# Seven half-size products for one more group: sums, a held-back unit and a moved load in a linear-attention and feed-forward kernel

## The chip, the core and the metric

The kernel runs on one core of a Trainium2 chip. The core has a matrix engine (TensorE, PE in the profile; its weight loads are PEld), a vector engine (VectorE, DVE), a scalar engine (ScalarE, ACT), GpSimd (POOL) and SyncE (SP), which here issues nearly all DMAs. Each engine works through its own instructions in program order and waits on semaphores for the others. The metric is the device time of one execution in microseconds.

## The reference

Eight batches of attention with a linear kernel, followed by a two-layer feed-forward network on all 4608 tokens:

```python
def phi(x, c, s):                       # c, s: cos and sin of the position
    r = np.maximum(x, 0.0)
    return np.concatenate([r * c, r * s], axis=-1)
q_p, k_p = phi(q, cos_w, sin_w), phi(k, cos_w, sin_w)   # (8, 8, 576, 64) -> (..., 128)
kv  = np.einsum('bhsf,bhsd->bhfd', k_p, v)
z   = np.sum(k_p, axis=2)
num = np.einsum('bhsf,bhfd->bhsd', q_p, kv)
den = np.einsum('bhsf,bhf->bhs', q_p, z)[..., None] + 1e-06
x   = (num / den).transpose(0, 2, 1, 3).reshape(4608, 512)
h   = x @ w_in                          # 512 -> 2048
g   = np.maximum(0.01 * h, h)
out = g @ w_out                         # 2048 -> 512
```

## The kernel before

The tokens are cut into nine groups of 512, counted from 0: groups 0 to 7 hold the first 512 tokens of batches 0 to 7, group 8 the 64 tokens that are left of every batch. Both weight matrices are kept in SBUF in 16 bits (`w1`, `w2`).

For every batch b the steps are: load k, v and q (`load_kv`, `load_main`, DMAs on SP's queue into a pool of five staging buffers); build k's features, 9 tokens with a cosine and a sine half each (`k_cos`, `k_sin`, L267 on VectorE or L265 on ScalarE, tile kp); cast v (`v_pairs`); sum k and v into kv on TensorE (`kv_sum`, L366, 72 small matmuls, with a copy on ScalarE); build q's features in four parts j (`q_prep`, tile qp) and transpose them by DMA in two halves (`q_transpose_dma`, L401); for each j multiply with kv (`num`, L432) and divide on VectorE (`divide`: den, rden, xs, L443 to L448); and transpose x by DMA (`x_transpose_dma`, L413). `num` and `kv_sum` share the one buffer of the PSUM pool `ps_n`.

For every group g the first product (`ffn1`, L504) has 16 units of four 512-wide matmuls. Two units fill one buffer of the pool `ps_h`, which has two, and ScalarE takes them through the leaky ReLU into the tile g (L512).

The second product has two forms. Groups below `G7` (3 before) take 16 units of four 512-wide matmuls (`ffn2`, L527), and each four units end in one copy from PSUM (`ffn2_out`) and a store. Groups from `G7` on use Strassen's scheme in Winograd's form: g is cut into quarters a11, a12, a21, a22 (two halves of the tokens, even and odd slices of the 2048 features), `w2` into b11, b12, b21, b22, and seven products of half the size take the place of eight. A product is two units of eight 256-wide matmuls (`ffn2s`, L610), 14 units in all, in the order 1, 6, 2, 7, 5, 4, 3. They accumulate in three chains, each in one bank of the pool `ps_o`, which has two banks: X holds products 1 and 2, Y holds 6, 7 and 4, Z holds 5 and 3. Between two products of a chain the sum so far is read out: t1 after product 1 (ScalarE), t2 after 6, t3 after 7 (adds on VectorE, L552), and an output quarter after 2 (ScalarE), 5, 4 and 3 (VectorE).

The operands are made on VectorE (`tt_op`, L552) by `g_sum`: S1 = a21 + a22 and S2 = S1 - a11; a21 becomes a11 - a21, and a12 becomes a12 - S2 after product 2. `weight_sum` makes T1, T2 and T4 in buffers of their own, and number 3 overwrites b12 in `w2` by b22 - b12, so that it has to stand behind the last group that uses `w2` as it is. Product 7 multiplies the new a21 with the new b12; product 6 is S2 by T2, product 5 S1 by T1.

The order is written out by hand. From group 1 on, a list of units (`order`, L856 to L871) holds for each g the units of the second product of g and those of the first product of g+1: `ahead` units of the second product first (15 for group 1, 8 for group 2, none for 3 to 7), the rest spread between the first product's units by `behind`. The n-th entry of the list of g has the place 16 g + 16 n / (length of the list). The steps of the batches have fixed places (L903 to L946), and `weave` puts a step ahead of the first unit whose place is not below the step's. So a list with more entries moves the steps against the units. Steps near the change: q of batch 4 from 30, k from 31, the `num` of batch 3 at 27.5, 28.6, 29.7 and 30.8, its x transpose at 31.4, q transposes of batch 4 at 31.6 and 33.2, loads of k and v of batch 5 at 31.7 and 33.4, v casts of batch 4 on ScalarE at 32.5 and 33.5, the kv sum of batch 4 at 36.

Of the kernel before, what the change touches and what calls it, by code (L numbers as in the profile page):

```python
# [20 lines left out]
def kernel(  # L21
# [27 lines left out]
    NFT = DFF // P  # L49
    NG = B + 1  # L50
    NE = D + 2
    G7 = 3

    ctx.enter_context(tc.manual_schedule())

# [21 lines left out]
    def psum(where, shape, dtype, name):  # L77
        p = {"h": ps_h, "o": ps_o, "n": ps_n}[where]
        return p.tile(shape, dtype, name=name, tag="ps_" + where)

    st = {}
    ACT, DVE, POOL = nc.scalar, nc.vector, nc.gpsimd
# [56 lines left out]
    for i in range(DFF // 512):  # L139
        for c in range(0, NKC, 2):  # L140
            n = 1 if i == 0 and c == 0 else 2
# [353 lines left out]
    def ffn1(g, m, lo=0, hi=MAIN, chunks=range(NKC), where="h"):  # L495

        if ("g", g) not in st:
            st["g", g] = gpool.tile([P, NFT, MAIN], dt.float16, name="g")
        if m % 2 == 0 and chunks[0] == 0 and lo == 0:
            st["h", m // 2] = psum(where, [P, 2, MAIN], dt.float32, "ps_h")  # L500
        xT = st["xT", g]
        ps = st["h", m // 2]
        for c in chunks:
            nc.tensor.matmul(  # L504
                ps[:, m % 2, lo:hi],
                lhsT=w1[m // 4, c][0][:, w1[m // 4, c][1], m % 4 : 512 : 4],
                rhs=xT[:, lo // P : hi // P, c, :],
                start=(c == 0 and lo == 0),
                stop=(c == NKC - 1 and hi == MAIN),
            )  # L510
        if m % 2 == 1 and chunks[-1] == NKC - 1 and hi == MAIN:
            nc.scalar.activation(st["g", g][:, m - 1 : m + 1, :], ps, AF.Lrelu)  # L512
            if g >= G7 and m == NFT - 1:
                for n in (1, 2):
                    g_sum(g, n, NPR // 2, NPR)

    def ffn2(g, i, eng=DVE):
        tt, part = divmod(i, 4)
        if part == 0 and ("ps_o", g, tt) not in st:
            st["ps_o", g, tt] = psum("o", [P, DM], dt.float32, "ps_o")  # L520
        ffn2_mm(g, tt, 4 * part, 4 * part + 4)
        if part == 3 and eng is not None:
            ffn2_out(g, tt, eng)

    def ffn2_mm(g, tt, lo, hi):
        for m in range(lo, hi):
            nc.tensor.matmul(  # L527
                st["ps_o", g, tt],
                lhsT=st["g", g][:, m, tt * P : (tt + 1) * P],
                rhs=w2[:, m, :],  # L530
                start=(m == 0),
                stop=(m == NFT - 1),
            )
# [5 lines left out]
    NPR, HT, HC = NFT // 2, 2 * P, DM // 2  # L539
# [11 lines left out]
    def tt_op(o, a, b, op):  # L551
        nc.vector.tensor_tensor(out=o, in0=a, in1=b, op=op)  # L552

    def weight_sum(n):
        b11, b12, b21, b22 = (w2q[:, e, c] for e in range(2) for c in range(2))
        if n == 1:
            tt_op(T1, b12, b11, ALU.subtract)
        elif n == 2:
            tt_op(T2, b22, T1, ALU.subtract)
        elif n == 4:  # L560
            tt_op(T4, b21, T2, ALU.subtract)
        else:
            tt_op(b12, b22, b12, ALU.subtract)

    def g_quarter(g, r, e, lo=0, hi=NPR):
        gv = st["g", g].rearrange("p (i e) t -> p e i t", e=2)
        return gv[:, e, lo:hi, r * HT : (r + 1) * HT]

    def g_sum(g, n, lo, hi):
        a11, a12, a21, a22 = (  # L570
            g_quarter(g, r, e, lo, hi) for r in range(2) for e in range(2)
        )
        if n == 1:
            tt_op(S1[:, lo:hi], a21, a22, ALU.add)
        elif n == 2:
            tt_op(S2[:, lo:hi], S1[:, lo:hi], a11, ALU.subtract)
        elif n == 3:
            tt_op(a21, a11, a21, ALU.subtract)
        else:
            tt_op(a12, a12, S2[:, lo:hi], ALU.subtract)  # L580

    def product(g, n):

        return {
            1: (g_quarter(g, 0, 0), w2q[:, 0, 0]),
            2: (g_quarter(g, 0, 1), w2q[:, 1, 0]),
            3: (g_quarter(g, 0, 1), w2q[:, 1, 1]),
            4: (g_quarter(g, 1, 1), T4),
            5: (S1, T1),
            6: (S2, T2),  # L590
            7: (g_quarter(g, 1, 0), w2q[:, 0, 1]),
        }[n]
# [4 lines left out]
    def ffn2s(g, u):  # L597
        n, tt = ORDER7[u // 2], u % 2
        a, b = product(g, n)
        key = "ps7", g, CHAIN[n]  # L600
        apart = g == NG - 1 and CHAIN[n] == "Z"
        if apart:
            key = *key, tt
        first = key not in st
        if first:
            where = "n" if g == NG - 1 and key[2] == "Y" else "h" if apart else "o"
            st[key] = psum(where, [P, 2, HC], dt.float32, "ps_7")
        ps = st[key]
        for i in range(NPR):
            nc.tensor.matmul(  # L610
                ps[:, tt],
                lhsT=a[:, i, tt * P : (tt + 1) * P],
                rhs=b[:, i],
                start=(first and i == 0),
                stop=(i == NPR - 1 and (apart or tt == 1)),
                skip_group_check=True,
            )
        if apart:
            part = slice(tt * HC, (tt + 1) * HC)
            osb = out_tile(g, HC)  # L620
            tt_op(osb, ps[:, tt], {5: t3, 3: t2}[n][:, part], ALU.add)
            store_tail(2 * (n == 5) + tt, 1, osb)
        if apart or tt == 0:
            return
        flat = ps.rearrange("p t c -> p (t c)")
        if n == 1:
            nc.scalar.copy(t1, flat)
        elif n == 6:
            tt_op(t2, flat, t1, ALU.add)
        elif n == 7:  # L630
            tt_op(t3, flat, t1, ALU.add)
        else:
            osb = out_tile(g, 512)
            if n == 2:
                nc.scalar.copy(osb, flat)
                g_sum(g, 4, 0, NPR)
            else:
                tt_op(osb, flat, {5: t3, 4: t1, 3: t2}[n], ALU.add)
            r, c = {2: (0, 0), 5: (1, 1), 4: (1, 0), 3: (0, 1)}[n]
            store_quarter(g, r, c, osb.rearrange("p (t c) -> p t c", t=2))  # L640

    def out_tile(g, n):
        if g == NG - 1:
            return stage.tile([P, n], dt.float32, name="osb", tag="stage")
        return opool.tile([P, n], dt.float32, name="osb", tag="osb")
# [29 lines left out]
    def ffn2_out(g, tt, eng):  # L675
        ps = st["ps_o", g, tt]
        osb = opool.tile([P, DM], dt.float32, name="osb", tag="osb")
        copy(eng, osb, ps)
        rows = out[g * S : g * S + MAIN, :].rearrange("(p j) d -> p j d", j=J)
        if g == 0:  # L680
            held.append((rows[:, tt, :], osb))
        else:
            nc.sync.dma_start(rows[:, tt, :], osb)
# [43 lines left out]
    for m in range(2):  # L727
        ffn1(0, m, 0, half, range(0, 1))
    num_half(0, 0, 1, None, ps)
    for m in range(2):  # L730
        ffn1(0, m, 0, half, range(1, 2))
# [37 lines left out]
    def f1(g, m, where="h"):  # L769
        return lambda: ffn1(g, m, where=where)  # L770

    def f2(g, i):
        return lambda: ffn2s(g, i) if g >= G7 else ffn2(g, i)

    steps = []

    def at(pos, f, *args):
        steps.append((pos, lambda: f(*args)))
# [26 lines left out]
    order = [(tt, part) for part in range(3) for tt in range(J)]  # L805
# [47 lines left out]
    for g in range(1, NG):  # L853
        last = 14 if g >= G7 else 16
        ahead = {1: 15, 2: 8, NG - 1: last}.get(g, 0)
        order = [f2(g, i) for i in range(ahead)]  # L856
        left = last - ahead
        behind = [
            0 if g == 1 else -(-16 * (k + 1) // left) - 1 for k in range(left)
        ]  # L860
        for i in range(16 if g + 1 < NG else 0):
            order.append(f1(g + 1, i))
            order += [f2(g, ahead + k) for k in range(left) if behind[k] == i]
            if i == 11 and g + 1 >= G7:
                order.append(lambda g=g: [g_sum(g + 1, n, 0, NPR // 2) for n in (1, 2, 3)])
        if g == G7 - 1:
            order.append(lambda: weight_sum(3))
        if g + 1 >= G7 and g + 1 < NG:
            order.append(lambda g=g: g_sum(g + 1, 3, NPR // 2, NPR))
        for n, u in enumerate(order):  # L870
            units.append((16 * g + 16 * n / len(order), u))  # L871

# [14 lines left out]
    def load_steps(b, pk, pv, pq):  # L887
        at(pk, load_kv, "k", k, b)
        at(pv, load_kv, "v", v, b)
        at(pq, load_main, "q", q, b)  # L890
# [30 lines left out]
    kv_steps(4, 31, 0.5, 36, ACT)  # L921
    out_steps(4, 37.3, 1.4, 1.2)

    load_steps(5, 31.7, 33.4, 25)
    for j in range(J):
        at(39 + 1.4 * j, q_prep, 5, j)
    for jp in range(2):
# [51 lines left out]
```

## Time and profile before

| | before |
|---|---|
| median of 3 runs | 285.25 us (285.19 to 285.26) |
| profiled execution | 285.09 us, span 283.3 us |
| busy: TensorE | 275.4 us, 97% of the span |
| busy: VectorE | 165.9 us, 59% |
| busy: ScalarE | 130.5 us, 46% |
| DMA | 57.53 MB, mean 203 GB/s |
| second product, 512-wide matmuls (L527) | 192, 379 ns each |
| second product, 256-wide matmuls (L610) | 672, 273 ns each |
| second product of group 2, first eight units | 97.19 to 104.10 us |

The durations of matmuls overlap their neighbours, since TensorE pipelines them: a unit of four 512-wide matmuls takes 0.86 us from start to start, not four times 379 ns. The chain of work that ended last counts them without the overlap, and is the view to cost TensorE by. In VectorE's timeline the next instruction also starts before the one ahead has quite ended, so a row is costed by the distance to the next row. A row gives its start, its duration, its engine and line, what it writes and reads, and in brackets how long the engine was idle ahead of it and what ended that.

### The profile page before, as it was taken

To read this page: it belongs to the slowest core of one execution; us is meant where nothing else is said; L and a number is where in the kernel's file an instruction comes from. 1 tells how busy PE (TensorE), PEld (TensorE's weight loads), DVE (VectorE), ACT (ScalarE), POOL (GpSimd) and SP (SyncE) were. 2 spreads that over 40 slices of the span, in tenths; PEclk is the share of its full clock that TensorE was granted. 3 is DMA by queue.
4 is the path that set the end of the run, shared out by engine and by line. 5 is a ranking of instruction groups with operands and counts; after the bars stand their busy time and mean duration, and the time that the engine had idled before them with its cause. 6 is when DMAs were issued, how large, how long until landed. Compare 5 with 4: busy or idle time off the path is not lost.

```text
span 283.3 us, 5818 instructions
## 1 busy us (share of the span) xinstructions
PE 275.4 (97%) x2442; PEld 177.7 (63%) x2442; DVE 165.9 (59%) x394; ACT 130.5 (46%) x175; POOL 11.5 (4%) x23
## 2 busy tenths in 40 slices
PE   7899999999999999999999999999999999999993
PEld 2585455555446555556777777767776677667882
DVE  5940597955993883856675567555556514324452
ACT  6856366572037524784493449343334242332300
POOL 2056000000000000000000000000000000000000
PEclk9999999999999999999999999999999999999999
DMA  7999999699999999799599919441496052111124
GB/s 225 335 384 415 377 398 372 182 221 306 238 247 308 382 192 280 238 210 328 204 191 353 265 49 185 99 125 40 108 190 149 2 111 76 38 39 36 38 79 110
DMA packets 78202, 57.53 MB, mean 203 GB/s; under 512 B 50400, under 2 KB 66784, under 8 KB 77792
## 3 DMA queue, kind: packets, MB, share of 16 engines
q1 hardware_dynamic: 77568, 56.63, 72.7%
q10 hardware_dynamic: 608, 0.52, 0.6%
q8 instruction: 19, 0.31, 0.5%
q14 instruction: 7, 0.06, 0.1%
HBM read 36.70 MB, written 9.44 MB: 163 GB/s over the span
## 4 chain that ended last, share of the span: by engine, by line
PE 93%; DMA 2%; SPq 1%; ACT 1%; DVE 1%; issue 0%; DVEq 0%
PE ps_h L504 44%; PE ps L610 26%; PE ps_o L527 15%; PE ps_kv L366 3%; PE ps_num L432 3%; DMA vst<-in_v_dram 2%; SPq L115 1%; PE ps_xth L484 1%; PE ps_qt L422 1%; SPq L105 1%; PE ps_numh L468 1%; PE ps_idle L187 0%; ACT qpT L273 0%; DVE xT L829 0%; DVE xs L448 0%
## 5 line engine op out<-in xcount | busy, mean ns | idle before, releaser
L504 PE MATMUL ps_h<-xT,w 128*128 128x512 f16 (+1 forms) x592 | 141.3, 374 | 0.1
L512 ACT ACTIVATE g<-ps_h 128x1024 f16<-128x1024 f32 x72 | 73.1, 1023 | 92.2 <-PE ps_h L504 92.1
L504 PEld LDWEIGHTS <-w 128*128 128x128 f16 x592 | 64.7, 114 | 41.1 <-DMA xT<-xs 0.3
L610 PEld LDWEIGHTS <-g 128*128 128x128 f16 x480 | 46.5, 98 | 14.1
L610 PE MATMUL ps<-w,g 128*128 128x256 f16 x384 | 48.8, 273 | 0.0
L527 PE MATMUL ps_o<-w,g 128*128 128x512 f16 x192 | 45.0, 379 | 0.0
L527 PEld LDWEIGHTS <-g 128*128 128x128 f16 x192 | 18.3, 98 | 20.5
L610 PE MATMUL ps<-T,ext 128*128 128x256 f16 x192 | 24.6, 273 | 0.0
L610 PEld LDWEIGHTS <-ext 128*128 128x128 f16 x192 | 18.5, 98 | 5.3
L443 DVE TENSOR_SCALAR den<-ps_num 128x8 f32<-128x8 f32 x28 | 4.6, 164 | 28.7 <-PE ps_num L432 28.5
L552 DVE TENSOR_TENSOR ext<-g 128x1024 f16<-128x1024 f16 x12 | 8.2, 687 | 22.1 <-ACT g L512 22.1
L552 DVE TENSOR_TENSOR ext<-ps,ext 128x512 f32<-128x512 f32 x12 | 8.3, 692 | 21.1 <-PE ps L610 21.1
L552 DVE TENSOR_TENSOR osb<-ps,ext 128x512 f32<-128x512 f32 (+1 forms) x20 | 12.7, 635 | 13.5 <-PE ps L610 13.4
L448 DVE TENSOR_TENSOR xs<-ps_num,rden 128x512 f16<-128x512 f32 x28 | 19.4, 691 | 1.0
L267 DVE TENSOR_SCALAR kp<-kst,sin_t 128x256 f16<-128x256 f32 x54 | 17.9, 347 | 0.0
L267 DVE TENSOR_SCALAR qp<-qst,cos_t 128x512 f16<-128x512 f32 (+1 forms) x34 | 15.5, 457 | 3.2 <-DMA qst<-in_q_dram 3.2
L265 ACT ACTIVATE kp<-kst,cos_t 128x256 f16<-128x256 f32 (+1 forms) x35 | 15.9, 489 | 1.2 <-DMA kst<-in_k_dram 1.2
L267 DVE TENSOR_SCALAR qp<-qst,sin_t 128x512 f16<-128x512 f32 (+1 forms) x34 | 15.5, 457 | 0.0
L432 PEld LDWEIGHTS <-qpT 128*128 128x128 f16 (+1 forms) x256 | 10.6, 101 | 5.4 <-issue 1.2
L610 PE MATMUL ps<-ext,g 128*128 128x256 f16 x96 | 12.3, 273 | 0.0
L432 PE MATMUL ps_num<-kv,qpT 128*128 128x66 f16 (+1 forms) x256 | 11.8, 194 | 0.0
L273 ACT CAST vm<-vst 128x1152 f16<-128x1152 f32 x10 | 11.3, 1147 | 0.3 <-DMA vst<-in_v_dram 0.3
(83 smaller groups left out, 182.5 us busy)
## 6 DMA issues: line engine op xcount, KB each, us to landing
out_dram<-osb SPq DMA_DIRECT2D x32, 256.0 KB, 2.9
qst<-in_q_dram SPq DMA_DIRECT2D x7, 1024.0 KB, 8.1
kst<-in_k_dram SPq DMA_DIRECT2D x6, 1152.0 KB, 9.5
vst<-in_v_dram SPq DMA_DIRECT2D x5, 1152.0 KB, 8.4
w2st<-in_moe_w_out_dram SPq DMA_DIRECT2D x3, 1024.0 KB, 13.4
ext<-in_moe_w_in_dram SPq DMA_DIRECT2D x4, 512.0 KB, 11.1
w1st<-in_moe_w_in_dram SPq DMA_DIRECT2D x3, 512.0 KB, 9.9
kst<-in_k_dram SPq DMA_DIRECT2D x2, 576.0 KB, 12.4
```

What stands on the lines that cost most here:

```text
L265: nc.scalar.activation(o, i, AF.Relu, scale=col)
L267: eng.tensor_scalar(out=o, in0=i, scalar1=0.0, scalar2=col, op0=ALU.max, op1=ALU.mult)
L273: nc.scalar.copy(o, i)
L366: nc.tensor.matmul(ps[:, o, (c - lo) * NE : (c - lo + 1) * NE], lhsT=st["kp", b][sl, c, j, :], rhs=vm[b % 2][sl, c, j, :], start=(j == 0), ...
L432: nc.tensor.matmul(ps[lo:hi, h // 4, (h % 4) * NE : (h % 4 + 1) * NE], lhsT=qpT[:, h, lo:hi], rhs=kv[b][:, h, :],)
L443: nc.vector.tensor_scalar_add(den.rearrange("p (a b) -> p a b", a=2), ps[:, :, D : 4 * NE : NE], 1e-6)
L448: nc.vector.tensor_tensor(out=xs, in0=ps[:, :, 0 : 4 * NE].rearrange("p a (b e) -> p a b e", e=NE)[:, :, :, 0:D], in1=rden.rearrange("p (a ...
L504: nc.tensor.matmul(ps[:, m % 2, lo:hi], lhsT=w1[m // 4, c][0][:, w1[m // 4, c][1], m % 4 : 512 : 4], rhs=xT[:, lo // P : hi // P, c, :], s ...
L512: nc.scalar.activation(st["g", g][:, m - 1 : m + 1, :], ps, AF.Lrelu)
L527: nc.tensor.matmul(st["ps_o", g, tt], lhsT=st["g", g][:, m, tt * P : (tt + 1) * P], rhs=w2[:, m, :], start=(m == 0), stop=(m == NFT - 1),)
L552: nc.vector.tensor_tensor(out=o, in0=a, in1=b, op=op)
L610: nc.tensor.matmul(ps[:, tt], lhsT=a[:, i, tt * P : (tt + 1) * P], rhs=b[:, i], start=(first and i == 0), stop=(i == NPR - 1 and (apart or ...
```

## The change

Group 2 joins the groups that use the seven half-size products, so `G7` is 2. `weight_sum(3)` moves from behind group 2 to behind group 1. The sums S1 and S2 of group 2 are made in three parts (feature pairs 0 to 3, 4 and 5, 6 and 7) after units 8, 12 and 15 of its first product, and the difference on a21 in one piece behind group 1's list. Unit 15 of group 1's second product is held back from behind unit 0 to behind unit 15 of group 2's first product, and its copy goes to ScalarE. For the groups from 3 on the sums stay as they were. The load of q of batch 5 moves from place 25 to 33.3, behind batch 3's x transpose at 31.4 and the load of k of batch 5. Of group 2's units, eight still stand ahead; six instead of eight are spread behind.

```diff
-    G7 = 3
+    G7 = 2
...
             if g >= G7 and m == NFT - 1:
                 for n in (1, 2):
-                    g_sum(g, n, NPR // 2, NPR)
+                    g_sum(g, n, 6 if g == G7 else 4, NPR)
...
     def f2(g, i):
-        return lambda: ffn2s(g, i) if g >= G7 else ffn2(g, i)
+        return lambda: ffn2s(g, i) if g >= G7 else ffn2(g, i, ACT if (g, i) == (1, 15) else DVE)
...
         behind = [
-            0 if g == 1 else -(-16 * (k + 1) // left) - 1 for k in range(left)
+            -(-16 * (k + 1) // left) - 1 for k in range(left)
         ]
         for i in range(16 if g + 1 < NG else 0):
             order.append(f1(g + 1, i))
             order += [f2(g, ahead + k) for k in range(left) if behind[k] == i]
-            if i == 11 and g + 1 >= G7:
-                order.append(lambda g=g: [g_sum(g + 1, n, 0, NPR // 2) for n in (1, 2, 3)])
-        if g == G7 - 1:
-            order.append(lambda: weight_sum(3))
+            for at_i, lo, hi, sums in (
+                ((8, 0, 4, (1, 2)), (12, 4, 6, (1, 2))) if g + 1 == G7 else ((11, 0, 4, (1, 2, 3)),)
+            ):
+                if i == at_i and g + 1 >= G7:
+                    order.append(
+                        lambda g=g, lo=lo, hi=hi, sums=sums: [g_sum(g + 1, n, lo, hi) for n in sums]
+                    )
         if g + 1 >= G7 and g + 1 < NG:
-            order.append(lambda g=g: g_sum(g + 1, 3, NPR // 2, NPR))
+            lo = 0 if g + 1 == G7 else NPR // 2
+            order.append(lambda g=g, lo=lo: g_sum(g + 1, 3, lo, NPR))
+            if g + 1 == G7:
+                order.append(lambda: weight_sum(3))
...
-    load_steps(5, 31.7, 33.4, 25)
+    load_steps(5, 31.7, 33.4, 33.3)
```

## The prediction

> **What bounds the kernel now.** I read the page first, its busy table and its chain.
>
> ```profile
> PE 275.4 (97%) x2442; PEld 177.7 (63%) x2442; DVE 165.9 (59%) x394; ACT 130.5 (46%) x175; POOL 11.5 (4%) x23
> ...
> PE 93%; DMA 2%; SPq 1%; ACT 1%; DVE 1%; issue 0%; DVEq 0%
> ```
>
> TensorE is the bound: the chain is 93% TensorE, so work taken from it is worth its full length and every stall put into it costs its full length. VectorE's 59% is an average; what counts is how far it runs behind where TensorE needs it. So next the chain in order of time, at the place of the change.
>
> ```profile
> 97.19 6.91 PE ps_o L527 x32
> 104.10 0.86 PE ps_h L504 x4
> 104.96 1.25 PE ps_kv L366 x72
> ...
> 130.32 0.87 PE ps L610 x8
> ```
>
> The first row is the eight second-product units of group 2 that stand ahead of group 3's first product: 6.91/8 = 0.864 us each, no gap after them. The last is one half-size unit, 0.87 us. Third, VectorE's timeline over the same stretch.
>
> ```profile
> 95.50 0.17 DVE L443 TENSOR_SCALAR den<-ps_num 128x8 f32<-128x8 f32 x1
> ...
> 95.94 0.69 DVE L448 TENSOR_TENSOR xs<-ps_num,rden 128x512 f16<-128x512 f32 x1
> 96.54 0.48 DVE L267 TENSOR_SCALAR qp<-qst,cos_t 128x512 f16<-128x512 f32 x1
> 96.94 0.48 DVE L267 TENSOR_SCALAR qp<-qst,sin_t 128x512 f16<-128x512 f32 x1
> 97.33 0.35 DVE L267 TENSOR_SCALAR kp<-kst,cos_t 128x256 f16<-128x256 f32 x1
> 97.60 0.34 DVE L267 TENSOR_SCALAR kp<-kst,sin_t 128x256 f16<-128x256 f32 x1
> ...
> 101.54 0.68 DVE L275 COPY osb<-ps_o 128x512 f32<-128x512 f32 x1
> ...
> 104.24 0.68 DVE L275 COPY osb<-ps_o 128x512 f32<-128x512 f32 x1
> ```
>
> From 95.5 to 104.9 VectorE never idles, and it is behind: the copy at 101.54 reads a unit that TensorE finished at 97.19 + 4 x 0.864 = 100.65. Rows follow each other every 0.395 us (qp), 0.263 (kp), 0.61 (a copy or add of 512 from PSUM). That lateness costs nothing now: the other bank takes the next two blocks. Order is that of the program, here and everywhere in this timeline.
>
> **The change part by part.** *Products.* Sixteen units of 0.864 us go, fourteen of 0.868 come: 13.82 - 12.15 = 1.67 us less on TensorE, all on the path.
>
> *Sums and adds.* Group 2 gets S1 and S2 (parts 0-4, 4-6, 6-8), the difference on a21, the one on a12, and three output adds and two inner adds for three VectorE copies; the fourth group 1 copy goes to ScalarE. A sum of 1024 takes 0.69 us, one of 2048 takes 1.22 (1.13 to the next). The 512-wide parts have no row: on the line through these two, 0.16 + 0.53 per 1024, they take 0.42; ends 0.16 and 0.69. The early parts fall at 88 to 95 us, where VectorE idled 2.40, 1.72 and 0.86 us before rows at 88.68, 91.53 and 93.51; hidden. Without that cover they cost about 2 us. The late ones fall into the full stretch above.
>
> *The list of group 1 now has 36 entries instead of 32*, and its first-product units come 0.86 us earlier, so the steps of batch 3 land between other units. Division j=2 now follows j=1 with one unit between, 0.26 + 0.86 = 1.12 us, through the single ps_n buffer. A division takes from the matmuls' start at 91.07 to xs's end at 92.66, 1.59 us. TensorE waits 0.5 us (ends 0 and 0.5; I take 0.5, its own rows).
>
> *The add t2 in VectorE's queue* is what decides. In the eight units ahead, products 1, 6, 2, 7 stand back to back. Product 7 accumulates into the bank of product 6 (chain Y), so it must wait until VectorE's t2 add has read that bank; it also needs the a21 difference and the weight difference. Walk the queue: group 2's last first-product unit now has unit 15 of group 1 and the division j=3 of batch 3 behind it (0.86 + 0.26), so it ends at 97.19 - 1.12 + 0.5 = 96.6. ScalarE's activation, 1.02, ends at 97.65. The last S1 and S2 parts wait for it and VectorE with them: 97.65 to 98.45. Behind them, in the order of the new list, with the pitches above:
> - division j=3 (0.20 + 0.24 + 0.61): 99.5
> - qp of j=1, 0.79: 100.3; kp pair 0, 0.53: 100.8
> - a21 difference, 1.13: 101.95; kp pair 1: 102.5; weight difference, 1.13: 103.6
> - qp of j=2: 104.4; kp pair 2: 104.9; qp of j=3: 105.7
> - kp pairs 3, 4, 5: 107.3
> - t2: ends 107.95.
>
> TensorE starts product 1 at 97.19 + 0.5 = 97.7 and is through six units at 102.9. It waits 5.1 us. Ends: 0, if the queue is not in the way, and 5.6, if the 512-wide parts take 0.69; I take 5.1, from rows of the same stretch.
>
> *Behind that wait* everything on TensorE moves back, and VectorE too has more in its queue: kp pairs 6 and 7, the a12 difference (1.13), kp pair 8, to 110.65. TensorE ends product 7 at 108.0 + 1.74 = 109.7, and the kv sum of batch 4, now directly behind it, needs pair 8 from its 17th matmul of 72, 0.28 us in: 0.65 us (ends 0 and 0.9). Later, from group 3's unit 5 to the kv sum of batch 5, TensorE has 12 units instead of 13, while ScalarE's nine cosines and two casts stay. Before, that sum started at 125.43 and the last cosine, at 125.05 for 0.51, ended behind it: no cover is left. 0.7 us, between 0 and 0.87.
>
> *Unit 15 held back* costs no work; it gives the activation and sums 0.86 us of cover. Its copy on ScalarE, 0.59 us, goes between the activation and the cast of v, before product 6 wants the bank at 99.4.
>
> *The t1 copy* on ScalarE stands behind the first v cast (1.15), which started at 98.56 on a late load: ends 100.3, product 2 needs it at 99.4 + 1.7 = 101.2. If v came a microsecond later, product 2 would wait, and the wait for t2 would be shorter by the same.
>
> *q of batch 5 moved* past x of batch 3, both q transposes of batch 4 and k of batch 5 on SP's queue. It and k swap staging buffers; both are free by then. The x transpose was issued at 96.72 and took 7.1 us with that load in flight (median 4.6). It now waits for division j=3, 99.5, and lands at 104.1 to 106.6, while group 3 starts after 111: hidden. The load now stands behind the second q transpose, whose input is ready at 105.7 and which held SP 5.62 us: issued by 111.4. This window's q loads took 6.6 and 14.3 us; 6.6, the one with less in flight, gives 118, about when VectorE reaches its first qp (before: 113.11, plus the delay, 118.5). At 14.3 VectorE would stand still for 7 us and TensorE, which wants ps_n at 122, for about 5. I take 0.
>
> Sum: -1.67 + 0.5 + 5.1 + 0.65 + 0.7 = +5.3 us on the profiled execution's 285.09 (span 283.3): 290.4. The median of the runs, 285.25, stands 0.16 higher, so 290.5.
>
> **The rivals.** *The clock falls during the wait.* Matmuls after an idle stretch run slow for a while: the kernel's first 14 idle products took
>
> ```profile
> 1.19 4.61 PE L187 MATMUL ps_idle<-blank 128*128 128x512 f16 x14 [1.19 <-DVE blank L182]
> ```
>
> against 14 x 0.216 + 0.16 = 3.2 us at the pitch of the chain above, 1.4 us more. The same after a 5.1 us wait, part of it covered by the 0.65 us wait for the kv sum, adds 0.75 to 1.4: 291.3 to 291.9. Against: no TensorE gap of before is over 1.2 us, so no row shows a loss after one, and the page's PEclk has nines throughout. [...]
>
> *VectorE reaches t2 in time* (the other side). Place: product 7's first unit. If t2 ended by 102.9, only the 0.5 and at most the 0.7 would be left: 285.25 - 1.67 + 0 to 1.2 = 283.6 to 284.8, middle 284.2. It decides as soon as t2 ends before about 103.4, which needs 4.6 us of the qp and kp work to run ahead of the late sums. For: q and k of batch 4 are there by 94.56 and 97.33, and VectorE idles some 0.6 us before the S1 part. Against: the order in the rows.
>
> *Product 7 waits for the weight difference alone* (103.6, 0.7 us), t2 being early by some order I misread: 285.25 - 1.67 + 0.7 + 1.2 = 285.5, no change.
>
> *q of batch 5 is late as well*: 14.3 us, some 2 to 5 more, 292.5 to 295.
>
> **How the numbers follow.** Forecast 60%, 290.5 (its own range 288.3 to 291.4: the product wait at 4.7 without the three small ones, or all at their upper ends). Clock 20%. VectorE in time 12%. Weight difference alone 3%. Late q 5%. The range 288.3 to 292.4 leaves out the last three, 20%. A change under 0.2% (0.6 us) can't be told from none here. Slower: 60 + 20 + 5 = 85%; within it 3%, plus 1% of the 12% at its upper end, 4%; faster 11%.
>
> **What would show it.** In the profile after: one TensorE wait of about 5 us near 103 to 108, released by VectorE's add from PSUM at L552, with product 7 behind it; ps_num waiting 0.5 us near 94; small waits at two kv sums; t2 ending near 108. Half units at 0.868 and PEclk below nine behind the wait would tell the clock apart. Wrong if TensorE runs through from 97.7 to 104.6: then the queue's order was not the one I walked, or VectorE's work there is shorter than its rows before.

## The result and the profile after

The changed kernel takes 291.72 us (median of 4 runs, 291.05 to 292.09) against 285.22 beside it: 1.0226 times as long, with an interval of 1.0205 to 1.0246. It is slower by 6.5 us. The profiled execution took 291.47 us, with a span of 289.7. The first two lines are the page's busy table and its chain by engine, the third is its row of the granted TensorE clock:

```profile
PE 277.3 (96%) x2490; PEld 183.6 (63%) x2490; DVE 171.1 (59%) x402; ACT 132.1 (46%) x178; POOL 11.5 (4%) x23
...
PE 87%; DVE 5%; ACT 3%; DMA 2%; SPq 1%; issue 1%; DVEq 0%
...
PEclk9999999999999997999999999999999999999999
```

The chain was 93% TensorE and is 87% now: VectorE's part has grown from 1% to 5% and ScalarE's from 1% to 3%. The clock row has a 7 where it had a 9, in the 16th of 40 slices, that is between 108.6 and 115.9 us. The chain in order of time shows VectorE's part and the slow product behind it (ScalarE's part lies between 125.7 and 131.8 us, ahead of the kv sum of batch 5):

```profile
99.35 0.69 DVE xs L448
100.05 0.79 DVE qp L267 x2
100.83 0.53 DVE kp L267 x2
101.36 1.13 DVE g L552
102.49 0.53 DVE kp L267 x2
103.02 1.13 DVE w L552
...
105.47 0.79 DVE qp L267 x2
106.26 1.58 DVE kp L267 x6
107.84 0.61 DVE ext L552
108.45 0.04 issue
108.49 3.57 PE ps L610 x16
112.06 1.25 PE ps_kv L366 x72
```

Division j=3, q features, kp pairs, the a21 difference, the weight difference, and last the t2 add: the list that the prediction walked. The add ends at 108.44 and only then does product 7 start. Product 7's 16 matmuls take 3.57 us, where products 1, 6 and 2 take 1.74 each. TensorE's own timeline, with the wait in brackets, and the granted clock (the 1.00, 0.76, 0.50 ahead of the DMA share) by stretch:

```profile
94.88 0.41 PE L432 MATMUL ps_num<-kv,qpT 128*128 128x66 f16 x8 [0.45 <-DVE xs L448]
...
101.48 1.91 PE L610 MATMUL ps<-w,g 128*128 128x256 f16 x16
108.49 3.57 PE L610 MATMUL ps<-w,g 128*128 128x256 f16 x16 [5.11 <-DVE ext L552]
112.00 1.32 PE L366 MATMUL ps_kv<-vm,kp 64*128 64x66 f16 x72
...
130.85 0.40 PE L366 MATMUL ps_kv<-vm,kp 64*128 64x66 f16 x14
131.58 1.33 PE L366 MATMUL ps_kv<-vm,kp 64*128 64x66 f16 x58 [0.33 <-DVE kp L267]
132.84 1.49 PE L504 MATMUL ps_h<-xT,w 128*128 128x512 f16 x6
```

```profile
106.00:108.00 2.00, 0.00 (x0) 0.00 (x0) 2.00 (x8) 0.00 (x0) 0.00 (x0) 1.00 0.81 116
108.00:109.00 1.00, 0.51 (x3) 0.38 (x3) 1.00 (x4) 0.00 (x0) 0.00 (x0) 0.76 0.82 263
109.00:110.00 1.00, 1.00 (x7) 0.69 (x6) 1.00 (x3) 0.00 (x0) 0.00 (x0) 0.50 1.01 327
110.00:111.00 1.00, 1.00 (x6) 0.70 (x5) 1.00 (x3) 0.00 (x0) 0.00 (x0) 0.50 0.97 286
```

The wait is 5.11 us long, and behind it the clock stands at half for 3.4 us (108.5 to 111.9). The account on TensorE, up to the last block of half-size units (265.67 before, 272.70 after, 7.03 later): a start that came 0.36 later in this execution; -1.67 for the products; 0.45 at division j=2; 5.11 for t2; 1.83 for half clock (3.57 us for product 7 instead of 1.74); 0.74 at the kv sum of batch 5 (1.99 us from its first matmul to group 4's next unit, against 1.25 without a wait); sum 6.82, with 0.2 in small pieces. The span grew by only 6.4, since the last stores closed 0.6 sooner.

The questions for the experiments: is it VectorE's queue that makes the wait, and is it the add's place in it or the amount of work; is the idle stretch what halves the clock; and do the two other parts, the moved load and the held-back unit, cost anything by themselves?

### The profile page after: what moved, and what is told of

It is laid out like the page before. It is cut to its first block, busy times and chain, and to the rows that moved or that the text cites. A ratio compares the mean times of both kernels' runs of the same rounds, so it can differ in the third digit from the quotient of the medians.

```text
span 289.7 us, 5924 instructions
## 1 busy us (share of the span) xinstructions
PE 277.3 (96%) x2490; PEld 183.6 (63%) x2490; DVE 171.1 (59%) x402; ACT 132.1 (46%) x178; POOL 11.5 (4%) x23
## 4 chain that ended last, share of the span: by engine, by line
PE 87%; DVE 5%; ACT 3%; DMA 2%; SPq 1%; issue 1%; DVEq 0%
PE ps_h L504 42%; PE ps L610 28%; PE ps_o L527 9%; PE ps_kv L366 3%; PE ps_num L432 3%; DMA vst<-in_v_dram 2%; DVE kp L267 1%; SPq L115 1%; DVE qp L267 1%; ACT kp L265 1%; DVE xs L448 1%; ACT vm L273 1%; ACT g L512 1%; PE ps_xth L484 1%; PE ps_qt L422 1%
## 5 line engine op out<-in xcount | busy, mean ns | idle before, releaser
L610 PEld LDWEIGHTS <-g 128*128 128x128 f16 x560 | 55.0, 99 | 21.8 <-issue 5.3
L610 PE MATMUL ps<-w,g 128*128 128x256 f16 x448 | 58.3, 278 | 5.1 <-DVE ext L552 5.1
L527 PE MATMUL ps_o<-w,g 128*128 128x512 f16 x128 | 29.8, 379 | 0.0
L610 PE MATMUL ps<-T,ext 128*128 128x256 f16 x224 | 28.5, 273 | 0.0
L610 PEld LDWEIGHTS <-ext 128*128 128x128 f16 x224 | 21.6, 98 | 5.8
L552 DVE TENSOR_TENSOR ext<-g 128x1024 f16<-128x1024 f16 (+1 forms) x15 | 9.8, 652 | 24.6 <-ACT g L512 24.6
L552 DVE TENSOR_TENSOR osb<-ps,ext 128x512 f32<-128x512 f32 (+1 forms) x23 | 14.8, 642 | 13.9 <-PE ps L610 13.8
L552 DVE TENSOR_TENSOR ext<-ps,ext 128x512 f32<-128x512 f32 x14 | 9.7, 692 | 22.0 <-PE ps L610 22.0
L527 PEld LDWEIGHTS <-g 128*128 128x128 f16 x128 | 12.1, 98 | 13.0
L610 PE MATMUL ps<-ext,g 128*128 128x256 f16 x112 | 14.4, 273 | 0.0
L373 ACT CAST kv<-ps_kv 128x528 f16<-128x528 f32 (+1 forms) x8 | 4.4, 544 | 17.0 <-PE ps_kv L366 17.0
```

Of the source, the lines that this page charges most:

```text
L373: nc.scalar.copy(kv[b].rearrange("p (c o) e -> p o c e", o=2)[:, :, lo:hi, :], ps[:, :, 0 : n * NE].rearrange("p o (c e) -> p o c e", c=n),)
L527: nc.tensor.matmul(st["ps_o", g, tt], lhsT=st["g", g][:, m, tt * P : (tt + 1) * P], rhs=w2[:, m, :], start=(m == 0), stop=(m == NFT - 1),)
L610: nc.tensor.matmul(ps[:, tt], lhsT=a[:, i, tt * P : (tt + 1) * P], rhs=b[:, i], start=(first and i == 0), stop=(i == NPR - 1 and (apart or ...
```

## The experiments

**Filling the gap.** Theory: the idle stretch halves the clock. Rival: product 7 is slow for another reason.

```diff
     def ffn2s(g, u):
+        if g == G7 and u == 6:
+            ps = psum("h", [P, 2, MAIN], dt.float32, "ps_fill")
+            for _ in range(22):
+                nc.tensor.matmul(ps[:, 0], lhsT=T1[:, 0, 0:P], rhs=T1[:, 0:2, :])
```

> The changed kernel, with 22 matmuls of 512 columns on weights (result not used) put on TensorE between product 2 and product 7 of group 2. At 0.216 us each they take 4.75 us of the 5.11 us in which TensorE waits for the t2 add, so they should move nothing by themselves. Theory: after the wait TensorE runs at half clock for 3.5 us (granted clock 0.50, product 7 takes 3.57 us instead of 1.74), and the idle stretch is the cause. Then here the mean granted clock is 1.000, product 7 takes 1.74 us, the kv sum of batch 4 meets the wait of up to 0.65 us that was covered, and the time falls from 291.7 to 290.0 to 290.6. Rival: product 7 is slow for another reason (its weights, the wait itself): product 7 stays at 3.5 us and the time at 291.7 or above.

290.15 us (290.08 to 290.42), 1.0173 times before (1.0158 to 1.0188). TensorE's timeline (this kernel's lines lie four further down):

```profile
103.02 4.91 PE L601 MATMUL ps_fill<-T 128*128 128x512 f16 x22
108.30 1.91 PE L614 MATMUL ps<-w,g 128*128 128x256 f16 x16 [0.36 <-DVE ext L552]
110.14 0.43 PE L366 MATMUL ps_kv<-vm,kp 64*128 64x66 f16 x16
111.01 1.06 PE L366 MATMUL ps_kv<-vm,kp 64*128 64x66 f16 x56 [0.44 <-DVE kp L267]
```

Matmuls in the gap, whose result nothing uses, make the kernel faster. Product 7 is back at its full rate (1.91 us in this view for 16 matmuls, as for products 1, 6 and 2, which start 1.74 us apart), the mean clock is 1.000, and the kv sum's wait that half clock had covered appears, 0.44 us, after 16 of its 72 matmuls. Half clock cost the difference of the medians, 1.57 us, net of that wait which it had covered. The rival falls.

**The add first, the same work ahead of the kv sum.** Theory A: the place of the add in the queue is the cost. Theory B: VectorE has too much to do before the kv sum.

```diff
-    q_steps(4, 30, 0.8, 0.8)
-    kv_steps(4, 31, 0.5, 36, ACT)
+    for j, p in enumerate((30, 30.8, 33.6, 33.7)):
+        at(p, q_prep, 4, j)
+    at(31.6, q_transpose_dma, 4, 0)
+    at(33.75, q_transpose_dma, 4, 1)
+    kv_steps(4, 33.8, 0.15, 36, ACT, vs=(32.5, 1))
...
-    load_steps(5, 31.7, 33.4, 33.3)
+    load_steps(5, 31.7, 33.9, 33.85)
```

> The changed kernel with the same VectorE work in another order: the q features j=2 and 3 and all kp pairs of batch 4 stand behind the t2 add, still ahead of the kv sum of batch 4. Theory A (the place of the add alone costs the time): product 7 waits only for the weight difference and the add, about 0.4 us, nothing takes the place of the wait, and the time is about 291.7 - 4.7 - 1.8 = 285 us. Theory B (VectorE has some 5 us too much work between group 2's last activation and the kv sum, and the add was only the first to feel it): product 7 waits 0.4 us, and the kv sum of batch 4 then waits 5 to 5.7 us for the last kp pair, which still ends near 110.6; the clock falls behind that wait instead, so that the time stays at 290.5 to 292.

291.84 us (291.72 to 292.24), no better than the change as it was. TensorE's timeline:

```profile
103.36 1.91 PE L610 MATMUL ps<-w,g 128*128 128x256 f16 x16 [0.38 <-DVE ext L552]
105.47 0.20 PE L366 MATMUL ps_kv<-vm,kp 64*128 64x66 f16 x2 [0.21 <-DVE kp L267]
...
109.23 0.23 PE L366 MATMUL ps_kv<-vm,kp 64*128 64x66 f16 x2 [1.46 <-DVE kp L267]
...
110.81 1.72 PE L366 MATMUL ps_kv<-vm,kp 64*128 64x66 f16 x56 [0.29 <-DVE kp L267]
112.46 4.37 PE L504 MATMUL ps_h<-xT,w 128*128 128x512 f16 x12
```

Product 7 waits 0.38 us instead of 5.11, and the kv sum then takes its pairs one by one as VectorE makes them, the last at 110.81. Its nine waits come to 3.8 us, not to the 5 to 5.7 that were expected. In the changed kernel VectorE had made that pair by 111.14 (its row starts at 110.79 and takes 0.35). Theory A falls, B stands. And the clock halved here too (mean 0.987; 12 matmuls of group 3 take 4.37 us, 2.78 in the kernel with the filled gap), although no gap in this stretch is longer than 1.46 us:

```profile
107.00:109.00 2.00, 0.41 (x4) 0.19 (x4) 2.00 (x5) 0.00 (x0) 0.00 (x0) 0.98 0.79 232
109.00:111.00 2.00, 0.90 (x14) 0.50 (x16) 2.00 (x8) 0.00 (x0) 0.00 (x0) 0.50 0.96 288
```

**The same wait in two halves.** To see what sort of gap halves the clock: three of the items in front of the add go behind it, so that two waits of about 3 us stand on the two sides of product 7.

```diff
-    q_steps(4, 30, 0.8, 0.8)
-    kv_steps(4, 31, 0.5, 36, ACT)
+    for j, p in enumerate((30, 30.8, 33.55, 33.6)):
+        at(p, q_prep, 4, j)
+    at(31.6, q_transpose_dma, 4, 0)
+    at(33.65, q_transpose_dma, 4, 1)
+    kv_steps(4, 31.02, 0.5, 36, ACT, vs=(32.5, 1))
...
-    load_steps(5, 31.7, 33.4, 33.3)
+    load_steps(5, 31.7, 33.75, 33.7)
```

> The changed kernel with the q features j=2 and 3 and kp pair 5 of batch 4 moved from ahead of the t2 add to behind it (still ahead of the kv sum). The VectorE work in front of the kv sum is the same, so TensorE's waiting is the same in total, but in two pieces of about 3 us (product 7, then the kv sum) with product 7's 1.74 us of work between. [...]

291.59 us (291.20 to 291.69), where the changed kernel took 291.72 and the kernel with the filled gap 290.15. TensorE's timeline, then the clock:

```profile
106.02 1.91 PE L610 MATMUL ps<-w,g 128*128 128x256 f16 x16 [3.00 <-DVE ext L552]
107.85 0.36 PE L366 MATMUL ps_kv<-vm,kp 64*128 64x66 f16 x12
108.65 0.20 PE L366 MATMUL ps_kv<-vm,kp 64*128 64x66 f16 x2 [0.43 <-DVE kp L267]
110.31 0.20 PE L366 MATMUL ps_kv<-vm,kp 64*128 64x66 f16 x2 [1.46 <-DVE kp L267]
```

```profile
110.00:111.00 1.00, 0.36 (x12) 0.26 (x14) 1.00 (x4) 0.00 (x0) 0.00 (x0) 1.00 1.05 391
111.00:112.00 1.00, 1.00 (x56) 1.00 (x50) 0.38 (x1) 0.00 (x0) 0.00 (x0) 0.71 1.24 185
112.00:113.00 1.00, 1.00 (x9) 0.36 (x4) 0.00 (x0) 0.60 (x1) 0.00 (x0) 0.50 1.28 291
```

A gap of 3.00 us, 1.74 us of full work and some thin work and short waits after it: the clock still stands at 1.00 in product 7, and falls at about 111.4. So a single gap as long as the 5.11 us of the changed kernel is not needed. What this kernel, the one with the add first and the changed kernel have in common is several microseconds in which TensorE does little, not one gap of a certain length.

**The load of q alone, and the load put back.** Two kernels: the kernel before with only this load moved, and the changed kernel with only this load at its old place.

```diff
# the kernel before:
-    load_steps(5, 31.7, 33.4, 25)
+    load_steps(5, 31.7, 33.4, 33.3)
# the changed kernel:
-    load_steps(5, 31.7, 33.4, 33.3)
+    load_steps(5, 31.7, 33.4, 25)
```

> The kernel before with the load of q of batch 5 moved to place 33.3 and nothing else. In the kernel before this load was in flight when batch 3's x transpose was issued at 96.72 and took 7.1 us, the weight load of group 3's first unit idling 0.3 us. If the load is hidden in both places, the time is 285.2 within 0.3 us. If the late q holds up VectorE and through it ps_n, as it would at a landing of 14.3 us, the time rises by 1 to 5 us; if the x transpose was worth anything, it falls by up to 0.3.

> The changed kernel with the load of q of batch 5 back at place 25, as before. Forecast of the prediction: the moved load is hidden, so the time stays within 0.3 us of 291.7 (its own spread is 291.05 to 292.09). If the late q costs something on VectorE and in ps_n, it falls by that; if the early load makes v of batch 4 late for ScalarE or x of batch 3 late for group 3, it rises: v's cast would then start after 98.5, and the t1 copy behind it after 99.9.

Alone: 286.32 us (285.97 to 286.43), 1.0037 times before (1.0024 to 1.0050), 1.2 us slower by the medians. Put back: 291.43 us (291.24 to 292.12), its median within the spread of the changed kernel. VectorE's timeline of the first of the two:

```profile
116.38 0.49 DVE L267 TENSOR_SCALAR qp<-qst,cos_t 128x512 f16<-128x512 f32 x1 [3.08 <-DMA qst<-in_q_dram]
116.78 0.48 DVE L267 TENSOR_SCALAR qp<-qst,sin_t 128x512 f16<-128x512 f32 x1
117.18 0.34 DVE L267 TENSOR_SCALAR kp<-kst,sin_t 128x256 f16<-128x256 f32 x1
117.44 0.16 DVE L443 TENSOR_SCALAR den<-ps_num 128x8 f32<-128x8 f32 x1
```

VectorE stands 3.08 us on the late q, with a division queued behind it, and TensorE waits 1.0 us for the one buffer of `ps_n`. In the changed kernel the first qp of batch 5 runs at 120.22 with no wait for its load: the long stall ahead of it covers the late load, so moving it there costs nothing and putting it back gains nothing.

**The held-back unit alone**, in the kernel before:

```diff
-        return lambda: ffn2s(g, i) if g >= G7 else ffn2(g, i)
+        return lambda: ffn2s(g, i) if g >= G7 else ffn2(g, i, ACT if (g, i) == (1, 15) else DVE)
...
-            0 if g == 1 else -(-16 * (k + 1) // left) - 1 for k in range(left)
+            -(-16 * (k + 1) // left) - 1 for k in range(left)
```

> The kernel before with unit 15 of group 1's second product held back behind unit 15 of group 2's first product, its copy on ScalarE, and nothing else (group 2 keeps 16 full units). TensorE's work is the same. The division j=3 of batch 3 does not move behind the late sums, since there are none. Forecast: the same time, 285.2 within 0.3 us; at most the division j=2 waits 0.5 us for j=1, since the first product's units come 0.86 us earlier against the steps: up to 285.7.

284.77 us (median of 10 runs), 0.9988 times before (0.9979 to 0.9997): no loss. The gain of 0.3 us by the medians does not come from the stretch of the change: in both traces the last block of half-size units starts at 265.67.

**The whole stretch reordered.** If theory B holds, the change works once VectorE has only what product 7 needs in front of it, ScalarE takes part of the kp work (in the changed kernel its timeline shows it idle from 104.0 to 113.35), and the kv sum has a unit of other work ahead of it.

```diff
-    out_steps(3, 27.5, 1.1, 0.6)
+    for j, p in enumerate((27.3, 28.2, 29.5, 30.7)):
+        at(p, num, 3, j)
+    at(31, x_transpose_dma, 3)
...
-    q_steps(4, 30, 0.8, 0.8)
-    kv_steps(4, 31, 0.5, 36, ACT)
+    for j, p in enumerate((30, 30.8, 34.92, 35)):
+        at(p, q_prep, 4, j)
+    at(31.6, q_transpose_dma, 4, 0)
+    at(35.1, q_transpose_dma, 4, 1)
+    kv_steps(4, 33.55, 0.05, 36.3, ACT, range(2, 9), (32.5, 1))
...
-    load_steps(5, 31.7, 33.4, 33.3)
+    load_steps(5, 31.7, 33.4, 31.05)
...
-    kv_steps(5, 39.6, 0.65, 46, ACT, range(T), (42.5, 1.5))
+    kv_steps(5, 39.6, 0.65, 47.2, ACT, range(T), (42.5, 1.5))
```

> The changed kernel with the stretch relieved as theory B asks: behind the t2 add come the kp pairs of batch 4, with seven of its nine cosines on ScalarE; the q features j=2 and 3 and the a12 difference come behind them; the kv sum of batch 4 stands behind unit 0 of group 3's first product; the divisions of batch 3 have two units between them; q of batch 5 is loaded directly behind batch 3's x transpose; the kv sum of batch 5 stands one and a half units later. Theory B: product 7 waits about 0.4 us, the kv sum of batch 4 at most 0.3, the others nothing, the clock stays at 1.000, and the 1.67 us of the products come through but for 0.7 us: 284.0 to 284.6, faster than the kernel before. If seven products for group 2 have a cost that lies elsewhere than in VectorE's queue, it shows as a wait at another place and the time stays above 286.

290.77 us (290.19 to 291.01). The expectation failed, and TensorE's waits tell where; the rows are engine, line, whom it waited for, microseconds, times, longest:

```profile
PE ps_num L432 <- DMA qpT<-qp: 4.5, 2, 3.6
...
PE ps L610 <- ACT ext L627: 0.5, 1, 0.5
```

No wait for VectorE is left: its t2 add runs at 102.45 and the kp work is out of the way in time. The q transposes of batch 4 are late instead. SP's timeline and its DMA rows have them at 103.58 (9.1 us to landing), right behind the load of q, and at 112.24 (9.0), behind the loads of k and v. The clock halved again behind TensorE's wait of 3.58 us for the first (mean 0.990; the first eight half-size matmuls after it take 1.69 us to the next start, the next eight 0.88).

**The q load back at place 25**, the second q transpose ahead of the load of v, the q features j=2, 3 ahead of the a12 difference, the v casts behind the t1 copy:

```diff
-    for j, p in enumerate((30, 30.8, 34.92, 35)):
+    for j, p in enumerate((30, 30.8, 33.96, 33.98)):
...
-    at(35.1, q_transpose_dma, 4, 1)
-    kv_steps(4, 33.55, 0.05, 36.3, ACT, range(2, 9), (32.5, 1))
+    at(33.99, q_transpose_dma, 4, 1)
+    kv_steps(4, 33.55, 0.05, 36.3, ACT, range(2, 9), (33, 0.3))
...
-    load_steps(5, 31.7, 33.4, 31.05)
+    load_steps(5, 31.7, 34, 25)
```

> The reordered kernel again, with the DMA queue put right: the load of q of batch 5 back at place 25 (its own q transposes waited 9.1 us behind it in the reordered kernel), the second q transpose of batch 4 ahead of the load of v of batch 5, the q features j=2 and 3 ahead of the a12 difference, and the v casts of batch 4 behind the t1 copy. Theory B and nothing else: product 7 waits about 0.4 us, the kv sum of batch 4 at most 0.3, no q transpose is waited for, the clock is 1.000, and the time is 283.8 to 284.6, faster than before. Rival: with seven products the stretch has too little room for the DMAs as well; then a transpose is still waited for and the time stays above 285.5.

284.17 us (median of 12 runs, 283.92 to 286.26), 0.9979 times before (0.9963 to 0.9995). It came out in the expected range, and the waits left in the stretch are 0.4 us for t2 and 0.2 us for batch 3's x.

**Room for the last two waits.** The kv sum and the divisions of batch 3 stand a unit earlier, the q features j=1 ahead of the late sums.

```diff
-    kv_steps(3, 20.7, 0.4, 27, ACT, vs=(24.6, 0.8))
-    for j, p in enumerate((27.3, 28.2, 29.5, 30.7)):
+    kv_steps(3, 20.7, 0.4, 26.1, ACT, vs=(23, 0.5))
+    for j, p in enumerate((27, 27.9, 28.85, 30.1)):
         at(p, num, 3, j)
-    at(31, x_transpose_dma, 3)
+    at(30.6, x_transpose_dma, 3)
...
-    for j, p in enumerate((30, 30.8, 33.96, 33.98)):
+    for j, p in enumerate((30, 30.05, 33.96, 33.98)):
         at(p, q_prep, 4, j)
-    at(31.6, q_transpose_dma, 4, 0)
+    at(31.2, q_transpose_dma, 4, 0)
```

> The kernel with the q load put back, with the two waits that were left in it attacked: the kv sum of batch 3 and its four divisions stand one unit earlier (v of batch 3 cast earlier on ScalarE), so that division j=3 and with it the x transpose no longer follow group 2's last S1 and S2 parts, and the q features j=1 of batch 4 fill VectorE's idle 0.87 us ahead of those parts. There the t2 add ended after product 2 by 0.4 us and group 3's first product waited 0.2 us for x. Expected: both waits gone, at most 0.25 us at division j=3, clock 1.000, 283.3 to 284.0, that is the 1.67 us of the products whole or nearly so. Against: if the remaining distance to 283.5 lies in the products themselves or in the start of the kernel, the time stays at 284.1 or above.

284.41 us (median of 11 runs, 284.13 to 285.15), 0.9968 (0.9958 to 0.9979): both waits are gone, but the expected 283.3 to 284.0 did not come, and against the step before the intervals overlap. One new wait has taken their place:

```profile
PE ps_num L432 <- DMA qpT<-qp: 1.1, 1, 1.1
```

The division j=2 of batch 4 now comes before its transpose, which landed 8.64 us after its issue, behind the load of k of batch 5.

**That load behind the transpose, in two steps.**

```diff
# first
-    load_steps(5, 31.7, 34, 25)
+    load_steps(5, 33.995, 34, 25)
# second, on top of the first
-    kv_steps(5, 39.6, 0.65, 47.2, ACT, range(T), (42.5, 1.5))
+    kv_steps(5, 40.2, 0.6, 47.2, ACT, range(T), (42.5, 1.5))
```

> The kernel with the room made, and in it the load of k of batch 5 moved behind the second q transpose of batch 4. In the kernel without this step that transpose, issued behind the k load, landed 8.64 us after its input was ready, and the division j=2 of batch 4 waited 1.1 us for it; every other wait of the stretch was gone. Expected: the transpose lands in 4.5 to 6 us, the wait is gone, and the time is 283.3 to 283.9, 1.4 to 1.9 below the kernel before. Against: k of batch 5 then lands near 116 and ScalarE's first cosine of batch 5, which stands ahead of an activation, may hold up group 3's first product; then a wait for ps_h or for the kv sum of batch 5 shows and the time stays at 284.2 or above.

285.25 us, 1.0000 times before (0.9991 to 1.0009), where 283.3 to 283.9 was expected. The transposes land in 4.5 to 4.8 us, as expected, but now k is late: VectorE's first sine of batch 5 waits for it ahead of a division, as the late q did above.

```profile
PE ps_num L432 <- DVE xs L448: 1.6, 1, 1.6
```

> The kernel with k of batch 5 behind the second q transpose, and in it the k features of batch 5 started at place 40.2 instead of 39.6, behind the division j=2 of batch 4. In the kernel without this step k landed at 116.3, VectorE's first sine stood ahead of that division, and the division j=3 waited 1.6 us for it through ps_n; ScalarE's wait of 2.86 us for the same load cost TensorE nothing. Expected: that wait gone as well and no other left in the stretch, 285.25 - 1.6 = 283.7 (283.4 to 283.9). Against: if the wait only moves on (to the division j=3's own readers or to the kv sum of batch 5), the time stays above 284.5, and this stretch has no room for the saving.

283.47 us (283.36 to 283.81), 0.9943 times before (0.9930 to 0.9957), 1.73 us faster. Three rows of TensorE's waits of this kernel; none in the stretch of the change is longer than these:

```profile
PE ps_h L504 <- DMA xT<-xs: 0.2, 1, 0.2
PE ps_kvh L312 <- DVE g L275: 0.2, 1, 0.2
PE ps_xth L484 <- DVE xs L448: 0.2, 1, 0.2
```

This version beats both kernels. How much of its gain is the saving of two units, 1.67 us in the prediction, is not shown apart: the same reordering with the full units kept for group 2 was not run. By the profiled executions, from the kv sum of batch 2 to the last block of half-size units takes 203.22 us (61.21 to 264.43) against 204.37 before (61.30 to 265.67), 1.15 us less; with the 0.25 us that TensorE still waits for batch 3's x it would be 1.4. The rest of the 1.73 us lies outside this stretch or between executions.

## Why the prediction was right, and where it was off

The direction and the mechanism held, and the range (288.3 to 292.4) held the time, but the likeliest case did not come alone: the time, 291.72, lies in the case with the falling clock (291.3 to 291.9), which had 20%. With the clock kept, by the filled gap, it is 290.15, against a sum of 290.5.

- *Products*, -1.67 us: about right, but no run shows it by itself. The 0.868 us for a half-size unit is a little low: products 1, 6 and 2 of the changed kernel take 1.745 us per two units, and at 0.872 the saving is 1.6.
- *The division j=2*, 0.5 us: 0.45 in the trace.
- *The add t2*, 5.1 us: 5.11. The add was to end at 107.95; it ended at 108.44 in an execution that started 0.36 us later. The unseen 512-wide sums were put at 0.42 us and took 0.41 to 0.43. Walking the queue by the distances between the old rows was enough. But the add's place in the queue, which the prediction says decides, is only where the lateness shows first: with the add first, the kv sum waits instead and the time stays, so the cost is VectorE's work between group 2's last activation and the kv sum.
- *The kv sum of batch 4*, 0.65 us: 0 in the changed kernel, since half clock made product 7 last longer and covered it, as the prediction's clock rival said; 0.44 us where the clock is kept.
- *The kv sum of batch 5*, 0.7 us: 0.74, in the account above.
- *The clock.* This is the step that was off: a chance of 20%, the author's estimate, with the argument that no row of before shows a loss after a gap. No TensorE gap of before was over 1.2 us, so its silence was weak evidence against. It happened in every run of the changed kernel (mean clock 0.988 to 0.994, against 0.996 to 1.000 before), and cost 1.57 us by the filled gap, against 0.75 to 1.4 in the prediction. That figure came from the kernel's first 14 products, 4.61 us long, and they ran at a granted clock of 1.00 (0 to 8 us of before), so they show slow matmuls without a lowered clock. Mean clocks of 0.994 and 0.988 over some 290 us answer to about 3.5 and 7 us at half rate, an estimate; the two runs at 0.994 took 291.05 and 291.47 us, the two at 0.988 took 291.96 and 292.09. In the profiled execution the clock stood at 0.50 for 3.4 us. It fell too in the two kernels with shorter gaps, longest 3.00 and 1.46 us.
- *The unit held back*, nothing: right (0.9988 alone). *The moved q load*, nothing: right in the changed kernel, where it issued at 112.29 (at the latest 111.4 was expected), landed 6.7 us later, and VectorE reached it at 120.22. The cover is the stall itself: without the stall the late load costs 1.2 us, which the prediction did not say.

## What to carry to other kernels

Before work is taken from the bound engine, list what the other engine has queued between the last input it gets and the first output that is waited for, and add it up by the distances between the rows of the old trace; here that gave 5.1 us against 5.11. When such a wait is long, moving the waited-for item to the front only hands the wait on to the next reader: take work out of the stretch, or give the bound engine other work to do meanwhile. Price a stall like this one on TensorE with a half-rate stretch behind it (here 3.4 us at half rate behind a wait of 5.11 us, 1.57 us of the time), and after each repair look again for what is late next: here a transpose behind a load, then the load behind the transpose.

## What the runs showed of the hardware

With the add first, the TensorE clock fell to half (0.50) without any TensorE wait over 1.46 us in the stretch, while the kv sum ran in bursts of two small matmuls every 0.53 us; in the kernel with the filled gap it had stayed at full rate (1.00) through 4.91 us of matmuls whose results nobody used. In the split kernel it fell at about 111.4, more than 5 us after the 3.00 us gap had ended. Where it fell, TensorE had done little since its last full work: from the end of product 7 it was busy for 1.0 of 3.65 us with the add first (105.27 to 108.92) and for 1.3 of 3.5 us in the split kernel (107.93 to 111.4), and in the changed kernel not at all from the end of product 2 on (103.4 to 108.5). In the split kernel the clock was still 1.00 at the end of the 3.00 us gap and through product 7's 1.91 us behind it. What in these stretches decides was not shown. Half rate lasted 3.4 us in the changed and the split kernel (108.5 to 111.9 and 111.4 to 114.8), and 6.8 us with the add first (108.9 to 115.7).

Of the q transposes of batch 4, those without a load issued just ahead of them on the same queue landed in 4.3 us (before) and 4.8 us (changed), in 4.5 and 4.8 us in the kernel with k behind the second, and in the last kernel in 4.5 us for the first and 4.8 us as the median of both; those issued less than 3 us behind a load of 1024 or 1152 KB took 9.2 us (before), 7.7 us (changed), 9.1 and 9.0 us (reordered) and 8.64 us (the kernel with the room made).
